# A gated-attention kernel followed by a gelu MLP: one running loop over all batches, no squares on GpSimd, transposing loads issued from SyncE, and buffers of the second phase that wait tile by tile

## The chip, the cores and the metric

One core of a Trainium2 chip runs the whole program. The metric is the time of one execution on the device in microseconds (us), median of several; the profile is of one such execution. A trace's span is some 2 us under the time of its run.

Engines in the profile: PE is TensorE (matmuls), PEld its weight loads, DVE is VectorE, ACT ScalarE, POOL GpSimd, SP SyncE, which issues DMAs. A letter q behind a name is the engine's queue of issues. L225 is line 225 of that kernel, so the same statement has another number in another kernel.

## The reference, cut to what matters

```python
# u, v: (8, 3008, 256)   z: (8, 3008, 64)   w_in: (256, 2048)   w_out: (2048, 256)
scores = (z @ z.transpose(0, 2, 1)) / 3008
attn = np.maximum(scores, 0.0) ** 2
x = (u * (attn @ v)).reshape(8 * 3008, 256)
h = x @ w_in
out = (h / (1 + np.exp(-1.702 * h))) @ w_out
```

## The kernel before: the parts that matter

The first phase works batch by batch. A batch has 72 iterations: two score matmuls (each on 64 rows, so z must lie on partitions 0 to 63 and again on 64 to 127), a relu with eviction (four in five on ScalarE, one in five on VectorE), a square (one in four on GpSimd), and, six iterations later, eight O matmuls.

```python
for b in range(B):
    for k in range(NIT + DPIPE):                  # 72 + 6: the last six only drain
        ...                                       # casts of V for b + 1 at k = 2, 6, 10, 14
        if k == NIT + 1: emit_zt_tr(b + 1, 0)     # 12 transposes into a buffer of the scores
        elif k == NIT + 2: emit_zt_ev(b + 1, 0)   # ScalarE: to ZT, partitions 0 to 63
        elif k == NIT + 3: emit_zt_tr(b + 1, 1)
        elif k == NIT + 4: emit_zt_ev(b + 1, 1)
        elif k == NIT + 5: emit_zt_dup(b + 1)     # DMA: copy to partitions 64 to 127
        if k < NIT: ...                           # sc = scores(k), two buffers
        if 0 <= k - 1 < NIT:
            ...                                   # r = relu(sc): VectorE if tcount % 5 == 0
            if POOL_SQ_EVERY and tcount % POOL_SQ_EVERY == 0:      # 4
                pool.tensor_tensor(ap_, r, r, ALU.mult)
            else:
                dve.tensor_tensor(ap_, r, r, ALU.mult)
        if k - DPIPE >= 0: ...                    # O += ap_ @ V; every 12th: X = O * u on VectorE
    sp.dma_start(xdram[...], X)                   # cut
```

The second phase takes 47 blocks of 512 tokens. Its input XT comes by transposing DMAs from xdram, issued from ScalarE; the first four blocks' (eight DMAs) run already in the second batch of the first phase, as soon as their X is stored.

```python
with (tc.tile_pool(name="pb", bufs=2) as pb, ...):   # takes the place of the first phase's pools
    load_xt(0, act)
    for tb in range(NTB + 1):
        load_xt(tb + 1, act)
        for fg in range(NFG):        # 8 groups: 4 matmuls to hg, sigmoid on ACT, GT = hg * tsg on DVE
            ...
        ...                          # 64 matmuls GT @ W2 of block tb - 1 to yps, ysb, store
```

By default a pool that is opened where others were waits for all users of those.

The names in the profile: ZT is the transposed z, ztp its transposes, sc the scores, r their relu, ap_ the square, O the products with V, X is O * u; hg is h, tsg its sigmoid, GT their product, yps the sums of the output, ysb their copy. The drain is the last six iterations of a batch, in which no new scores are made.

## Time and profile before

| | before |
|---|---|
| time, median of the first 4 runs | 1549.83 us (1549.45 to 1550.1) |
| span of the trace | 1547.7 us |
| first phase, first real scores to last O | 32.7 to 855.7 us |

The share of the whole span that TensorE is busy (95%) hides that it is full inside batches and stands for much of the time between them; the lines that show it are in the prediction. One more list matters, who made TensorE wait in the whole run: columns are total us, times, longest us.

```profile
PE sc L217 <- DMA ZT<-ZT: 43.1, 8, 16.7
...
PE hg L289 <- DVE GT L297: 8.7, 2, 7.9
PE sc L217 <- ACT r L232: 7.6, 10, 1.1
PE sc L217 <- DVE r L230: 3.2, 6, 1.0
```

The copy of ZT leads by far; 16.7 of its 43.1 us are in the start, the rest at the seven borders.

### The profile page before, as it was taken

The page shows a single profiled execution, that of the slowest core. Times are in us where ns is not written, and L with a number is a line of the kernel's source. Part 1 is how long each engine was busy: PE and PEld are TensorE (multiplying, and loading weights), DVE is VectorE, ACT ScalarE, POOL GpSimd, SP SyncE. Part 2 cuts the span into 40 slices and gives each one's busy share as a digit, 9 for nine tenths or more (in the row PEclk, how much of TensorE's full clock was granted, in tenths as well). Part 3 has the DMA queues.
Part 4 walks back from the last instruction along what each step waited for, and adds up shares of the span by engine and source line. Part 5 has one row for each costly group of instructions (what it writes and reads, how often), then busy time and mean ns, then how long its engine had stood idle before and what let it go on. Part 6 is the DMA issues. An engine that isn't in the chain of part 4 may idle for free.

```text
span 1547.7 us, 24671 instructions
## 1 busy us (share of the span) xinstructions
PE 1465.9 (95%) x10464; PEld 917.8 (59%) x10464; DVE 1116.6 (72%) x1117; ACT 892.0 (58%) x869; POOL 282.6 (18%) x152
## 2 busy tenths in 40 slices
PE   2998998999989999999999799999999999999998
PEld 1564564664646656656566466666666666666666
DVE  3875786777767767677687577777777777777775
ACT  2765665666656666566566455565555555555553
POOL 1332332333323323333333000000000000000000
PEclk9998999998989999999999899999999999999999
DMA  9916315115142021121200212111111211211211
GB/s 305 262 32 175 58 40 164 42 48 156 40 121 85 26 78 42 37 68 40 78 29 26 54 55 62 48 59 59 54 57 55 62 49 55 62 49 56 61 35 55
DMA packets 175422, 113.66 MB, mean 73 GB/s; under 512 B 77776, under 2 KB 174032, under 8 KB 175056
## 3 DMA queue, kind: packets, MB, share of 16 engines
q1 hardware_dynamic: 123376, 95.56, 20.9%
q10 hardware_dynamic: 51136, 12.33, 3.9%
q0 software_dynamic: 800, 4.19, 0.8%
q8 instruction: 82, 1.34, 0.4%
q14 instruction: 28, 0.23, 0.1%
HBM read 59.64 MB, written 36.96 MB: 62 GB/s over the span
## 4 chain that ended last, share of the span: by engine, by line
PE 89%; DMA 5%; DVE 2%; ACT 2%; issue 1%; ACTq 1%; SPq 0%; POOL 0%; DVEq 0%; POOLq 0%
PE O L252 34%; PE hg L289 22%; PE yps L314 21%; PE sc L217 11%; DMA ZT<-ZT 2%; ACT r L232 1%; DMA zst<-in_z_dram 1%; DMA xdram<-X 1%; PE ztp L132 1%; DMA w1s<-in_moe_w_in_dram 1%; ACTq L85 1%; DVE r L230 1%; ACT ZT L139 0%; DVE X L260 0%; DVE GT L297 0%
## 5 line engine op out<-in xcount | busy, mean ns | idle before, releaser
L232 ACT ACTIVATE r<-sc 128x1024 f16<-128x1024 f32 x461 | 467.6, 1023 | 300.8 <-PE sc L217 294.4
L296 ACT ACTIVATE tsg<-hg 128x1024 f16<-128x1024 f32 x376 | 379.6, 1023 | 286.8 <-PE hg L289 182.7
L297 DVE TENSOR_TENSOR GT<-hg,tsg 128x1024 f16<-128x1024 f32 x376 | 447.2, 1221 | 114.0 <-ACT tsg L296 111.9
L289 PE MATMUL hg<-XT,W 128*128 128x512 f16 x1504 | 372.8, 380 | 10.1 <-DVE GT L297 8.7
L314 PE MATMUL yps<-W,GT 128*128 128x256 f16 x3008 | 374.1, 273 | 0.0
L314 PEld LDWEIGHTS <-GT 128*128 128x128 f16 x3008 | 294.2, 98 | 94.0
L217 PE MATMUL sc<-ZT 64*128 64x512 f16 x1152 | 236.9, 400 | 55.0 <-DMA ZT<-ZT 43.1
L289 PEld LDWEIGHTS <-W 128*128 128x128 f16 x1504 | 146.6, 98 | 152.5 <-issue 28.2
L217 PEld LDWEIGHTS <-ZT 64*128 64x128 f16 x1152 | 57.4, 93 | 187.1 <-issue 138.1
L230 DVE TENSOR_SCALAR r<-sc 128x1024 f16<-128x1024 f32 x115 | 139.9, 1217 | 26.9 <-PE sc L217 26.7
L320 DVE TENSOR_SCALAR ysb<-yps 128x512 f32<-128x512 f32 x94 | 64.4, 685 | 64.9 <-PE yps L314 64.9
L260 DVE TENSOR_TENSOR X<-O,ru 128x1024 f16<-128x1024 f32 x48 | 58.5, 1218 | 27.6 <-PE O L252 27.6
L139 ACT ACTIVATE ZT<-ztp 64x1536 f16<-64x1536 f16 x16 | 23.0, 1442 | 31.5 <-PE ztp L132 31.5
L110 DVE CAST zst<-zst 128x1536 f16<-128x1536 f32 x8 | 7.7, 959 | 35.9 <-PE ztp L132 21.5
L132 PE MATMUL ztp<-ident,zst 128*64 128x128 f16 x192 | 14.8, 233 | 11.1 <-DVE zst L110 11.1
L182 ACT ACTIVATE V<-vst 128x1536 f16<-128x1536 f32 x14 | 20.2, 1480 | 6.4 <-PE O L252 6.4
L132 PEld LDWEIGHTS <-zst 128*64 128x64 f16 x192 | 12.3, 118 | 14.0 <-DVE zst L110 11.1
L180 DVE CAST V<-vst 128x1536 f16<-128x1536 f32 x14 | 12.9, 956 | 0.0
L296 ACT ACT_TABLE_LOAD x1 | 1.3, 1283 | 13.5 <-DMA xdram<-X 13.5
L158 DVE CAST V<-vst 128x1536 f16<-128x1536 f32 x4 | 3.6, 954 | 7.5 <-DMA vst<-in_v_dram 7.5
L236 POOL TENSOR_TENSOR ap__186<-r 128x1024 f16<-128x1024 f16 x1 | 1.9, 1887 | 21.8 <-ACT r L232 21.8
L236 POOL TENSOR_TENSOR ap__1340<-r 128x1024 f16<-128x1024 f16 x1 | 2.3, 2323 | 15.3 <-ACT r L232 15.3
(1740 smaller groups left out, 1719.3 us busy)
## 6 DMA issues: line engine op xcount, KB each, us to landing
out_dram<-ysb SPq DMA_DIRECT2D x47, 512.0 KB, 2.9
vst<-in_v_dram SPq DMA_DIRECT2D x8, 2944.0 KB, 13.0
ru<-in_u_dram SPq DMA_DIRECT2D x40, 512.0 KB, 3.9
xdram<-X SPq DMA_DIRECT2D x8, 1472.0 KB, 7.7
zst<-in_z_dram SPq DMA_DIRECT2D x8, 736.0 KB, 6.4
ZT<-ZT SPq DMA_DIRECT2D x8, 384.0 KB, 6.2
ru<-in_u_dram SPq DMA_DIRECT2D x8, 384.0 KB, 3.4
w1s<-in_moe_w_in_dram POOLq DMA_DIRECT2D x1, 2048.0 KB, 10.4
```

Source lines behind the costliest of these rows:

```text
L132: pe.transpose(ztp[:DQK, jj, :], zst16[:, j, :], ident)
L139: act.activation(zts[b][:DQK, g * (NJ // 2) * P:(g + 1) * (NJ // 2) * P], ztp[:DQK], AF.Copy, scale=1.0)
L217: pe.matmul(sc[:, g, :], ZT[h0:h0 + DQK, j * P:(j + 1) * P], ZT[h0:h0 + DQK, isup * ISUP:(isup + 1) * ISUP], start=True, stop=True,)
L230: dve.tensor_scalar(r[:, :, :], sc[:, :, :], 0.0, csc, ALU.max, ALU.mult)
L232: act.activation(r[:, :, :], sc[:, :, :], AF.Relu, scale=csc)
L252: pe.matmul(O[:, ib, :], ap_[:, g, ib * P:(ib + 1) * P], V16[:, j, :], start=first, stop=last,)
L260: dve.tensor_tensor(X[:, isup * NIBS:(isup + 1) * NIBS, :], O, ru, ALU.mult)
L289: pe.matmul(hg[:, e, :TBC], W1[:, k, ff * P:(ff + 1) * P], XT[:, k, :TBC], start=(k == 0), stop=(k == NK - 1),)
L296: act.activation(tsg[:, :, :TBC], hg[:, :, :TBC], AF.Sigmoid, scale=1.702 / FSC)
L297: dve.tensor_tensor(GT[:, fg * FFG:(fg + 1) * FFG, :TBC], hg[:, :, :TBC], tsg[:, :, :TBC], ALU.mult,)
L314: pe.matmul(yps[:, s2, :], GT[:, ff, s * P:(s + 1) * P], W2[:, ff, :], start=(ff == 0), stop=(ff == NFF - 1),)
L320: dve.tensor_scalar(ysb[:, yy * 2:yy * 2 + ns2, :], yps[:, :ns2, :], 1.0 / FSC, None, ALU.mult)
```

## The change

Its intent: the pipeline runs on from batch to batch, with the next batch's ZT made early and in a buffer of O; GpSimd does no squares; the transposing loads leave ScalarE's queue; and the second phase's buffers wait only for the tiles whose place they take.

```diff
-POOL_SQ_EVERY = 4
+POOL_SQ_EVERY = 0
-            ztp = ps_sc.tile([P, NJ // 2, P], F16, name="ztp", tag="sc")
+            ztp = ps_o.tile([P, NJ // 2, P], F16, name="ztp", tag="O")
-        for b in range(B):
-            for k in range(NIT + DPIPE):
+        ZT_TR0 = 42
+        ZT_EV0 = 44
+        ZT_TR1 = 55
+        ZT_EV1 = 57
+        ZT_DUP = 58
+        for gk in range(B * NIT + DPIPE):
+            b0, k0 = divmod(gk, NIT)          # scores
+            ...
+            g1 = gk - 1                       # relu, square
+            g2 = gk - DPIPE                   # O, of the batch that g2 falls in
-        tc.tile_pool(name="pb", bufs=2) as pb,                  # and ps_h, ps_y
+        tc.tile_pool(name="pb", bufs=2, reuse_waits="tile") as pb,
-        load_xt(0, act)                                         # and load_xt(tb + 1, act)
+        load_xt(0, sp)
```

(The bodies of the loop are the same statements with other indices.)

More of the change, by code (lines that the diff above doesn't have):

```diff
@@ L168 @@
             dve.tensor_copy(W2, w2s)
-        for b in range(B):
-            _, V16, X, _casts = loads.pop(b)
-            ZT = zts.pop(b)
-            scs = [None] * (NIT + DPIPE)
-            aps = [None] * (NIT + DPIPE)
-            Os = [None] * (NIS + 1)
-            us = [None] * (NIS + 1)
-            for k in range(NIT + DPIPE):
-                if k % 4 == 2 and (b + 1) in loads and loads[b + 1][3]:
-                    o, i_ = loads[b + 1][3].pop(0)
-                    if (k // 4) % 2 == 0:
+        ZT_TR0 = 42
[3 more added lines that the diff above has]
+        ZT_DUP = 58
+        V16d = {}
+        Xd = {}
+        scs = {}
+        aps = {}
+        Os = {}
+        us = {}
+        for gk in range(B * NIT + DPIPE):
+            b0, k0 = divmod(gk, NIT)
+            if b0 < B:
+                if k0 == 0:
+                    _, V16d[b0], Xd[b0], _c = loads.pop(b0)
+                if k0 % 4 == 2 and (b0 + 1) in loads and loads[b0 + 1][3]:
+                    o, i_ = loads[b0 + 1][3].pop(0)
+                    if (k0 // 4) % 2 == 0:
                         dve.tensor_copy(o, i_)
@@ L182 @@
                         act.activation(o, i_, AF.Copy, scale=1.0)
-                if k == PRO_AT:
-                    emit_loads(b + 2)
-                if k == NIT + 1:
-                    emit_zt_tr(b + 1, 0)
-                elif k == NIT + 2:
-                    emit_zt_ev(b + 1, 0)
-                elif k == NIT + 3:
-                    emit_zt_tr(b + 1, 1)
-                elif k == NIT + 4:
-                    emit_zt_ev(b + 1, 1)
-                elif k == NIT + 5:
-                    emit_zt_dup(b + 1)
@@ L195 @@
-                for kq in ((k,) if k < NIT else ()):
-                    isup, jp = divmod(kq, NJP)
-                    if jp == 0:
-                        ru = pa.tile([P, NIBS, D], F32, name="ru", tag="ru")
-                        us[isup] = ru
-                        lo = isup * ISUP
-                        hi = min(S, lo + ISUP)
-                        nfull = (hi - lo) // P
-                        if nfull:
-                            sp.dma_start(
-                                ru[:, :nfull, :],
-                                u[b, lo:lo + nfull * P].rearrange("(n p) c -> p n c", p=P),
-                            )
-                        rem = (hi - lo) - nfull * P
-                        if rem > 0:
-                            sp.dma_start(ru[:rem, nfull, :], u[b, lo + nfull * P:hi].unsqueeze(1))
-                            dve.memset(ru[rem:, nfull, :], 0.0)
-                    sc = ps_sc.tile([P, 2, ISUP], F32, name="sc", tag="sc")
-                    scs[kq] = sc
-                    for g in range(2):
-                        j = 2 * jp + g
-                        h0 = g * DQK
+                if k0 == PRO_AT:
+                    emit_loads(b0 + 2)
@@ new lines @@
+                if k0 == ZT_TR0:
+                    emit_zt_tr(b0 + 1, 0)
+                elif k0 == ZT_EV0:
+                    emit_zt_ev(b0 + 1, 0)
+                elif k0 == ZT_TR1:
+                    emit_zt_tr(b0 + 1, 1)
+                elif k0 == ZT_EV1:
+                    emit_zt_ev(b0 + 1, 1)
+                elif k0 == ZT_DUP:
+                    emit_zt_dup(b0 + 1)
+                isup, jp = divmod(k0, NJP)
+                ZT = zts[b0]
+                if jp == 0:
+                    ru = pa.tile([P, NIBS, D], F32, name="ru", tag="ru")
+                    us[(b0, isup)] = ru
+                    lo = isup * ISUP
+                    hi = min(S, lo + ISUP)
+                    nfull = (hi - lo) // P
+                    if nfull:
+                        sp.dma_start(
+                            ru[:, :nfull, :],
+                            u[b0, lo:lo + nfull * P].rearrange("(n p) c -> p n c", p=P),
+                        )
+                    rem = (hi - lo) - nfull * P
+                    if rem > 0:
+                        sp.dma_start(ru[:rem, nfull, :], u[b0, lo + nfull * P:hi].unsqueeze(1))
+                        dve.memset(ru[rem:, nfull, :], 0.0)
@@ new lines @@
+                sc = ps_sc.tile([P, 2, ISUP], F32, name="sc", tag="sc")
+                scs[gk] = sc
+                for g in range(2):
+                    j = 2 * jp + g
+                    h0 = g * DQK
+                    pe.matmul(
+                        sc[:, g, :],
+                        ZT[h0:h0 + DQK, j * P:(j + 1) * P],
+                        ZT[h0:h0 + DQK, isup * ISUP:(isup + 1) * ISUP],
+                        start=True, stop=True,
+                    )
+            g1 = gk - 1
@@ new lines @@
+            if g1 >= 0 and g1 in scs:
+                sc = scs.pop(g1)
+                r = pr.tile([P, 2, ISUP], F16, name="r", tag="r")
+                tcount += 1
+                if DVE_RELU_EVERY and tcount % DVE_RELU_EVERY == 0:
+                    dve.tensor_scalar(r[:, :, :], sc[:, :, :], 0.0, csc, ALU.max, ALU.mult)
+                else:
+                    act.activation(r[:, :, :], sc[:, :, :], AF.Relu, scale=csc)
+                ap_ = pr.tile([P, 2, ISUP], F16, name="ap_", tag="ap_")
+                aps[g1] = ap_
+                if POOL_SQ_EVERY and tcount % POOL_SQ_EVERY == 0:
+                    pool.tensor_tensor(ap_, r, r, ALU.mult)
+                else:
+                    dve.tensor_tensor(ap_, r, r, ALU.mult)
@@ new lines @@
+            g2 = gk - DPIPE
+            if g2 >= 0 and g2 in aps:
+                b2, k2 = divmod(g2, NIT)
+                isup, jp = divmod(k2, NJP)
+                ap_ = aps.pop(g2)
+                V16 = V16d[b2]
+                if jp == 0:
+                    Os[(b2, isup)] = ps_o.tile([P, NIBS, D], F32, name="O", tag="O")
+                O = Os[(b2, isup)]
+                for g in range(2):
+                    j = 2 * jp + g
+                    for ib in range(NIBS):
+                        first = (jp == 0 and g == 0 and (ib % 2) == 0)
+                        last = (jp == NJP - 1 and g == 1 and (ib % 2) == 1)
@@ L217 @@
                         pe.matmul(
-                            sc[:, g, :],
-                            ZT[h0:h0 + DQK, j * P:(j + 1) * P],
-                            ZT[h0:h0 + DQK, isup * ISUP:(isup + 1) * ISUP],
-                            start=True, stop=True,
-                        )
-                k1 = k - 1
-                if 0 <= k1 < NIT:
-                    sc = scs[k1]
-                    scs[k1] = None
-                    r = pr.tile([P, 2, ISUP], F16, name="r", tag="r")
-                    tcount += 1
-                    if DVE_RELU_EVERY and tcount % DVE_RELU_EVERY == 0:
-                        dve.tensor_scalar(r[:, :, :], sc[:, :, :], 0.0, csc, ALU.max, ALU.mult)
-                    else:
-                        act.activation(r[:, :, :], sc[:, :, :], AF.Relu, scale=csc)
-                    ap_ = pr.tile([P, 2, ISUP], F16, name="ap_", tag="ap_")
-                    aps[k1] = ap_
-                    if POOL_SQ_EVERY and tcount % POOL_SQ_EVERY == 0:
-                        pool.tensor_tensor(ap_, r, r, ALU.mult)
-                    else:
-                        dve.tensor_tensor(ap_, r, r, ALU.mult)
@@ L239 @@
-                k2 = k - DPIPE
-                if k2 >= 0:
-                    isup, jp = divmod(k2, NJP)
-                    ap_ = aps[k2]
-                    aps[k2] = None
-                    if jp == 0:
-                        Os[isup] = ps_o.tile([P, NIBS, D], F32, name="O", tag="O")
-                    O = Os[isup]
-                    for g in range(2):
-                        j = 2 * jp + g
-                        for ib in range(NIBS):
-                            first = (jp == 0 and g == 0 and (ib % 2) == 0)
-                            last = (jp == NJP - 1 and g == 1 and (ib % 2) == 1)
-                            pe.matmul(
-                                O[:, ib, :],
-                                ap_[:, g, ib * P:(ib + 1) * P],
-                                V16[:, j, :],
-                                start=first, stop=last,
-                            )
-                    if jp == NJP - 1:
-                        ru = us[isup]
-                        dve.tensor_tensor(X[:, isup * NIBS:(isup + 1) * NIBS, :], O, ru, ALU.mult)
-                        Os[isup] = None
-                        us[isup] = None
@@ L263 @@
-            sp.dma_start(
-                xdram[b * S:b * S + S0].rearrange("(n p) c -> p n c", p=P),
-                X[:, :NJ - 1, :],
-            )
-            if SREM:
-                sp.dma_start(xdram[b * S + S0:(b + 1) * S].unsqueeze(1), X[:SREM, NJ - 1, :])
+                            O[:, ib, :],
+                            ap_[:, g, ib * P:(ib + 1) * P],
+                            V16[:, j, :],
+                            start=first, stop=last,
+                        )
+                if jp == NJP - 1:
+                    X = Xd[b2]
+                    ru = us.pop((b2, isup))
+                    dve.tensor_tensor(X[:, isup * NIBS:(isup + 1) * NIBS, :], O, ru, ALU.mult)
+                    del Os[(b2, isup)]
+                    if isup == NIS - 1:
+                        sp.dma_start(
+                            xdram[b2 * S:b2 * S + S0].rearrange("(n p) c -> p n c", p=P),
+                            X[:, :NJ - 1, :],
+                        )
+                        if SREM:
+                            sp.dma_start(xdram[b2 * S + S0:(b2 + 1) * S].unsqueeze(1), X[:SREM, NJ - 1, :])
+                        del Xd[b2], V16d[b2], zts[b2]
@@ L270 @@
     with (
-        tc.tile_pool(name="pb", bufs=2) as pb,
-        tc.tile_pool(name="ps_h", bufs=3, space=bass.MemoryType.PSUM) as ps_h,
-        tc.tile_pool(name="ps_y", bufs=2, space=bass.MemoryType.PSUM) as ps_y,
+        tc.tile_pool(name="pb", bufs=2, reuse_waits="tile") as pb,
+        tc.tile_pool(name="ps_h", bufs=3, space=bass.MemoryType.PSUM, reuse_waits="tile") as ps_h,
+        tc.tile_pool(name="ps_y", bufs=2, space=bass.MemoryType.PSUM, reuse_waits="tile") as ps_y,
     ):
         GTs = [None] * (NTB + 1)
-        load_xt(0, act)
+        load_xt(0, sp)
@@ L277 @@
         for tb in range(NTB + 1):
             if tb < NTB:
-                load_xt(tb + 1, act)
+                load_xt(tb + 1, sp)
                 TBC = TBCs[tb]
```

## The prediction

> **What bounds the kernel now.** The page first. Its busy line says that TensorE leads, so the question is where TensorE works at its own pace and where it waits.
>
> ```profile
> PE 1465.9 (95%) x10464; PEld 917.8 (59%) x10464; DVE 1116.6 (72%) x1117; ACT 892.0 (58%) x869; POOL 282.6 (18%) x152
> ...
> L236 POOL TENSOR_TENSOR ap__186<-r 128x1024 f16<-128x1024 f16 x1 | 1.9, 1887 | 21.8 <-ACT r L232 21.8
> ```
>
> No other engine is above 72%. GpSimd holds 144 of the 576 squares, at 1.9 to 2.4 us each. Second, busy time by stretches, cut at the batch borders: the inside of a batch (354 to 444) against a border (234 to 247), the join of the two phases (849 to 868) and the second phase. Columns are the length of the stretch, each engine's busy time with its instructions, then clock, DMA share and GB/s.
>
> ```profile
> 234.00:247.00 13.00, 7.63 (x74) 5.73 (x73) 4.30 (x6) 5.74 (x4) 1.89 (x1) 0.95 0.58 130
> ...
> 354.00:444.00 90.00, 90.00 (x678) 53.86 (x678) 70.26 (x73) 56.83 (x56) 33.96 (x18) 0.98 0.24 72
> ...
> 849.00:868.00 19.00, 9.78 (x73) 6.77 (x72) 4.71 (x6) 4.55 (x5) 1.99 (x1) 0.88 0.29 81
> 868.00:1530.00 662.00, 661.15 (x4386) 428.32 (x4385) 500.53 (x463) 375.73 (x373) 0.00 (x0) 1.00 0.18 54
> ```
>
> Inside a batch TensorE is busy all 90.00 of 90 us, while VectorE is at 78% and ScalarE at 63%: nothing done for those two can shorten it. At the border TensorE has only 7.63 of 13 us. Third, the chain of waits and the timeline, to see what the border is.
>
> ```profile
> 237.31 0.80 PE ztp L132 x12
> 238.13 1.45 ACT ZT L139
> 239.60 7.07 DMA ZT<-ZT
> 246.72 0.62 PE sc L217
> 247.37 1.24 DVE r L230
> ```
>
> ```profile
> 246.72 1.03 PE L217 MATMUL sc<-ZT 64*128 64x512 f16 x2 [5.37 <-DMA ZT<-ZT]
> ...
> 864.03 1.28 ACT L296 ACT_TABLE_LOAD   x1 [13.51 <-DMA xdram<-X]
> ...
> 867.65 6.56 PE L289 MATMUL hg<-XT,W 128*128 128x512 f16 x16 [7.90 <-DVE GT L297]
> ```
>
> The next batch's transposed z is made only while the pipeline drains: transposes, an eviction on ScalarE, then a copy to the other 64 partitions that takes 7 us to land, and TensorE stands 5.4 us for it. Then the pipeline of depth 6 fills again. At the join ScalarE's first sigmoid waits until 864 for the last store of X, although its data (hg) were ready at about 858; TensorE runs 12 matmuls ahead and then stands 7.90 us.
>
> The size of the borders. In the steady stretch eight O matmuls start at 268.30 and those twelve iterations later at 283.94, so 1.303 us an iteration; 72 of them are 93.8 us a batch, with the two transposes (2 x 0.8 us) 95.4. The second eviction of ZT, one a batch, starts at 130.91, 238.13, 342.74, 447.32, about 552.3, 653.01 and 754.18: the batches took 107.2, 104.6, 104.6, 105.0, 100.7 and 101.2 us, which is 11.8, 9.2, 9.2, 9.6, 5.3 and 5.8 over. The first batch (32.7 to 133.6) is 5.5 over, the last (756.9 to 855.7, no transposes) 5.0. Sum 61.4 us of 823. The largest has eight transposing DMA issues on ScalarE's queue in it, 1.1 to 1.8 us each, between 143 and 158.
>
> **What the Trainium skill says.** "SBUF — State Buffer", section "SBUF: two separate sides": VectorE and GpSimd share one port pair, as an exclusive lock, held for the whole instruction, also against a VectorE operation with two SBUF inputs. The trace agrees. A square on VectorE takes 0.68 us alone; the one that began at 203.96 took 2.21, because GpSimd's ran from 203.73 to 205.62. In sum the 432 squares on VectorE take 390.1 us, mean 0.903. "TensorE: Matmul & The Clock Gate", section "What's actually happening": after about 3.4 idle us the array falls to half its clock. The trace agrees: granted clock 0.74 in 133 to 140, and a pair of sc matmuls takes 0.61 to 1.03 us after the wait in place of 0.39. "ScalarE: Activation LUTs", section "What ACT_TABLE_LOAD costs": 1283 ns for any set; here 1283 ns, once at the join. "DMA: Bandwidth & Descriptors", section "Issuing engines are not separate DMA queues": another issuing engine saves only the sequencer's time. Here that is about 1.25 us of ScalarE for each of 94 transposing DMAs.
>
> **The change part by part.**
>
> 1. *Squares all on VectorE.* It gains 144 x 0.68 = 98 us and loses the blocking, 432 x (0.903 - 0.68) = 96 us. Net 2 us of busy time on an engine at 78% where TensorE sets the pace: 0 us.
>
> 2. *One loop over all batches.* An iteration of the next batch follows the last without a drain, and the squares of the last six are consumed beside the first scores of the next. Transposes move to iterations 42 and 55, the copy to 58: at 1.3 us an iteration it has 14 x 1.3 = 18 us, against 7 to land. What goes is the excess of the seven later batches, 61.4 - 5.5 = 55.9 us. The first batch's filling (5.5) and the 32.7 us before it stay. The transposes stay on TensorE, 0.8 us each.
>
> 3. *What comes back.* The work that hid in the border (two evictions of 1.44 us and two casts of 1.48 on ScalarE; two casts of 0.95 and one of 0.96 on VectorE) now stands between relus. Scores have two buffers, so relu has some 2.2 us from ready to needed and takes 1.02 or 1.22: a burst of 1.4 us costs at most some 0.4, and the engine catches up within three iterations (slack of 0.48 us an iteration on ScalarE). The transposes now take one of the two O buffers: at iteration 42 the next O can start only when VectorE has multiplied the last one out (1.22 us plus the queue ahead of it), covered by 0.86 of transposes and 0.43 of scores, so 0 to 1 us. The second set, at 55, finds a free buffer. Estimate from these: 1.5 us a batch, 7 x 1.5 = 10.5 us.
>
> 4. *Buffers of the second phase wait for the tiles whose place they take, not for the whole pools.* At the join, from the last O (855.7) to steady work (867.65), TensorE did 2.8 us of work: 9.2 lost. If the tsg and GT buffers do not lie on the X of the last batch, the path is one hg pair (0.9), perhaps the table load (1.28), sigmoid 1.02 and product 1.22, against 2.6 us of hg work that three buffers allow: 1 to 2 us lost, so 7.5 saved. If they do lie on it, GT still waits for the store and 1 to 2 is saved. I give the first three chances in four: 6 us.
>
> 5. *Transposing loads from SP.* The eight early ones leave ScalarE in the second batch; that gain is already in part 2. In the second phase they delay one sigmoid per block by 1.2 us, but then TensorE is in a run of 49 yps matmuls that needs no sigmoid: 0.
>
> Sum: 55.9 - 10.5 + 6 = 51.4, less 1549.8 gives 1498. The second phase (868 to the end, 680 us) is carried over unchanged.
>
> **The rivals.** *VectorE becomes the bound.* For it: it gets a third more squares and has 20% of the relus, every one able to hold a score buffer. Against: the blocking it sheds is as large as the work it takes, and what it does in an iteration is 0.68 + 1.22/5 + 1.22/12 = 1.03 of 1.30 us. Were it to cost 0.1 us an iteration, 58 us would be lost and the time would be about 1555. *A new wait takes the border's place.* For it: only two score and two O buffers, in order queues, and a cast of z that waits for the transposes: VectorE stood 4.8 us for it at 238.14, which is harmless in a drain and not in a running pipeline. At 5 us a batch in place of 1.5 the time is about 1522. Against: first batch casts, at 43 to 60, cost some 2 to 3 us in all. *The instruction order shifts in the second phase.* The product there runs back to back on VectorE (seven in 8.34 us) while TensorE alternates, and a block takes 14.35 us against 13.65 for 32 x 0.2133 and 64 x 0.1067 (my estimate from the row widths at the pace of the long runs). A ScalarE free of issues might save up to 0.7 x 47 = 33 us, giving 1465. Against: TensorE is in order and its order should be the same.
>
> **Range and chances.** Nearly all of 51 us is idle TensorE time that the timeline shows, and each batch has a term of its own, so the error is mainly part 3 (0.5 to 4 us a batch: minus 7 to plus 17 us) and part 4 (minus 2 to plus 5). That gives 1483 to 1516. The 2% line is 1519, so faster 0.92, same 0.07, slower 0.01.
>
> **What would show it.** Windows of 10 us over the borders should have TensorE at 95% and over, with no 5 us wait for ZT and the clock at 1.0; successive batches should be about 97 us apart; the wait list should lose "sc from DMA ZT" but for the first; squares on VectorE should show 576 at about 0.68 and GpSimd nothing after the start; the first sigmoid should begin within 2 us of the first hg. I am wrong in part 3 if TensorE shows waits for relu of more than 2 us a batch, in part 4 if the first sigmoid or product still ends its wait with the X store, and in part 5 if the blocks of the second phase are not 14.35 us apart.

## The result, and the profile after

| | before | after |
|---|---|---|
| time, median | 1549.45 us (13 runs) | 1483.74 us (1483.21 to 1484.78, 8 runs) |
| span of the trace | 1547.7 us | 1481.5 us |
| last O of the first phase ends | 855.67 us | 800.85 us |
| from there to the end | 692.00 us | 680.65 us |

The ratio is 0.9579 (95% interval 0.9569 to 0.9588). Ratios are the mean time of one kernel's fast runs over that of the other's of the same rounds, so not quite the ratio of the medians. The output is correct.

Of the 66.2 us between the spans, 54.8 came in the first phase and 11.4 after it. The prediction had 55.9 - 10.5 = 45.4 and 6. The engines' busy times of the changed kernel:

```profile
PE 1443.8 (97%) x10464; PEld 913.2 (62%) x10464; DVE 1110.3 (75%) x1261; ACT 891.1 (60%) x869; POOL 2.7 (0%) x8
```

VectorE executes 144 instructions more and is busy 6 us less. The stretches of the changed kernel, in the columns of those of before (the first crosses a batch border near 320, the third is the join):

```profile
234.00:334.00 100.00, 99.36 (x774) 61.31 (x772) 78.87 (x105) 67.70 (x66) 0.00 (x0) 1.00 0.37 102
...
634.00:734.00 100.00, 99.98 (x780) 61.67 (x779) 75.48 (x98) 64.45 (x63) 0.00 (x0) 1.00 0.19 54
...
800.00:824.00 24.00, 22.74 (x137) 13.15 (x136) 20.77 (x18) 16.26 (x16) 0.00 (x0) 1.00 0.32 87
```

Borders can no longer be seen: 99.36 us and more of 100, clock 1.00. What TensorE still waits for:

```profile
PE sc L225 <- DMA ZT<-ZT: 17.3, 1, 17.3
...
PE sc L225 <- ACT r L239: 1.7, 4, 0.7
PE hg L299 <- DVE GT L307: 0.7, 2, 0.4
```

Seven of the eight waits for ZT are gone; the one of the start stays. The last products O * u of the batches begin at 134.15, 230.60, 326.12, 422.25, 518.01, 614.06 and 710.26: batches of 95.5 to 96.5 us, on average 0.6 over the floor of 95.4 that I had worked out, where I had allowed 1.5. At the join, in the changed kernel's timeline:

```profile
795.71 1.28 ACT L306 ACT_TABLE_LOAD   x1
...
801.75 1.02 ACT L306 ACTIVATE tsg<-hg 128x1024 f16<-128x1024 f32 x1 [4.75 <-PE hg L299]
...
802.16 2.94 PE L299 MATMUL hg<-XT,W 128*128 128x512 f16 x12 [0.45 <-DVE X L269]
```

The table load lies beside the last O matmuls, the first sigmoid waits for its data alone, and TensorE stands at most 0.45 us at a time in place of 7.90.

So the direction is right, and 1483.74 lies inside the range of 1483 to 1516, but at its very edge. Some 15 us of gain came from where I had expected none. The experiments look for them.

### The profile page after: what moved, and what is told of

Its sections match the earlier page's. It is cut to its first block, busy times and chain, and to the rows that moved or that the text cites.

```text
span 1481.5 us, 24464 instructions
## 1 busy us (share of the span) xinstructions
PE 1443.8 (97%) x10464; PEld 913.2 (62%) x10464; DVE 1110.3 (75%) x1261; ACT 891.1 (60%) x869; POOL 2.7 (0%) x8
## 4 chain that ended last, share of the span: by engine, by line
PE 95%; DVE 2%; DMA 1%; ACT 1%; SPq 1%; issue 0%; ACTq 0%; DVEq 0%
PE O L260 37%; PE hg L299 23%; PE yps L324 22%; PE sc L225 12%; DMA zst<-in_z_dram 1%; PE ztp L132 1%; SPq L114 1%; ACT r L239 1%; DVE X L269 0%; DVE r L237 0%; DVE GT L307 0%; ACT V L190 0%; SPq L107 0%; DVE W L168 0%; DVE V L188 0%
## 5 line engine op out<-in xcount | busy, mean ns | idle before, releaser
L225 PE MATMUL sc<-ZT 64*128 64x512 f16 x1152 | 227.8, 389 | 19.6 <-DMA ZT<-ZT 17.3
L299 PEld LDWEIGHTS <-W 128*128 128x128 f16 x1504 | 145.9, 97 | 141.9 <-issue 17.8
L225 PEld LDWEIGHTS <-ZT 64*128 64x128 f16 x1152 | 55.9, 93 | 140.8 <-issue 120.8
L132 PE MATMUL ztp<-ident,zst 128*64 128x128 f16 x192 | 14.6, 231 | 11.4 <-DVE zst L110 11.1
L110 DVE CAST zst<-zst 128x1536 f16<-128x1536 f32 x8 | 7.6, 956 | 14.8 <-DMA zst<-in_z_dram 14.7
```

The source lines that it names most:

```text
L132: pe.transpose(ztp[:DQK, jj, :], zst16[:, j, :], ident)
L225: pe.matmul(sc[:, g, :], ZT[h0:h0 + DQK, j * P:(j + 1) * P], ZT[h0:h0 + DQK, isup * ISUP:(isup + 1) * ISUP], start=True, stop=True,)
L299: pe.matmul(hg[:, e, :TBC], W1[:, k, ff * P:(ff + 1) * P], XT[:, k, :TBC], start=(k == 0), stop=(k == NK - 1),)
```

## The experiments

Times are medians, beside the kernel before on the same chip. First each small part was added alone to the kernel before, then each taken alone out of the changed kernel.

**The squares.** Added to the kernel before:

```diff
-POOL_SQ_EVERY = 4
+POOL_SQ_EVERY = 0
```

> The kernel before with nothing changed but all squares on VectorE. Theory A (squares are neutral, TensorE sets the pace inside a batch): 1549 us less 0 to 3 us; the only place for a gain is the first 27 us after the start of the scores, where the changed kernel's TensorE did 176 matmuls in 33 to 60 us against 160. Theory B (GpSimd's blocking of VectorE is what the prediction missed, 9 us of it): 1540 or less. Theory C (VectorE becomes the bound): above 1555.

Measured 1546.01 us against 1549.47: 3.5 us (ratio 0.9973, interval 0.9962 to 0.9984). Close to theory A, a little over its range; TensorE does 178 matmuls between 33 and 60 us in place of 160. Now the same line put back into the changed kernel (0 to 4):

> The changed kernel with every fourth square on GpSimd again. Theory A (relu has slack enough by itself, so bursts cost nothing): 1484 to 1487. Theory B (the bursts of casts and evictions are harmless only because VectorE is no longer blocked for up to 1.6 us at a time): the 9 us of return that I predicted and did not find come back, 1490 to 1496.

Measured 1498.55 us, against 1483.74: 14.8 us, and at once the time that I had predicted for the whole change. Theory A falls, and theory B named too little. (TensorE's instruction order is the same but for a few lines.) In this kernel's trace, just after the border of the first batch, where the casts of V fall in:

```profile
140.94 2.47 POOL L243 TENSOR_TENSOR ap__1386<-r 128x1024 f16<-128x1024 f16 x1 [5.09 <-DVE r L237]
141.58 2.38 DVE L245 TENSOR_TENSOR ap__1401<-r 128x1024 f16<-128x1024 f16 x1
...
144.62 2.20 POOL L243 TENSOR_TENSOR ap__1449<-r 128x1024 f16<-128x1024 f16 x1 [1.20 <-ACT r L239]
144.98 2.38 DVE L245 TENSOR_TENSOR ap__1432<-r 128x1024 f16<-128x1024 f16 x1
147.29 1.21 DVE L237 TENSOR_SCALAR r<-sc 128x1024 f16<-128x1024 f32 x1
...
148.55 0.39 PE L225 MATMUL sc<-ZT 64*128 64x512 f16 x2 [1.56 <-DVE r L237]
```

Two squares on VectorE take 2.38 us each beside squares on GpSimd, where one takes 0.68 alone; the relu behind them in the same queue starts late; the scores have two buffers and TensorE waits 1.56 us for that relu. The same place in the changed kernel, without GpSimd:

```profile
141.17 0.68 DVE L245 TENSOR_TENSOR ap__1432<-r 128x1024 f16<-128x1024 f16 x1
...
142.90 1.22 DVE L237 TENSOR_SCALAR r<-sc 128x1024 f16<-128x1024 f32 x1
...
143.41 0.39 PE L225 MATMUL sc<-ZT 64*128 64x512 f16 x2
```

Over the run, TensorE's wait for VectorE's relu is this with GpSimd's squares, and 0.2 us in one wait without:

```profile
PE sc L225 <- DVE r L237: 10.1, 10, 2.4
PE O L260 <- DVE X L269: 1.8, 3, 0.7
...
PE ztp L132 <- DVE X L269: 1.3, 2, 0.7
```

The waits for X rise from 0.7 to 3.1 us (O and transposes together). No wait of TensorE for a square of GpSimd is in the list. The longest one, 2.43 us, stands behind a cast of V on VectorE that took 2.64 us in place of 0.95, so casts are held up as well as squares. The spans differ by 15.1 us: TensorE's idle time grew by 11.9, about what these waits add (12.3), and its busy time by 3.2 (1447.0 against 1443.8). Matmuls did take longer after that longest wait: the granted clock was 0.62 from 340 to 342 us. Batches are 96.7 to 99.9 us apart.

Is it the blocking, or that a square of 1.9 us comes late to its own O matmuls? In the next run VectorE does all squares, and GpSimd works on something that nobody needs.

```diff
                     dve.tensor_tensor(ap_, r, r, ALU.mult)
+                if tcount % 4 == 0:
+                    scr = pr.tile([P, 2, ISUP], F16, name="scr", tag="scr", bufs=2)
+                    pool.tensor_tensor(scr, r, r, ALU.mult)
```

> The changed kernel, all squares on VectorE as in it, and GpSimd squares every fourth r a second time into a scratch tile that nobody reads; the result is right. If GpSimd's squares cost time because they keep VectorE waiting (a square of 0.69 us that took 2.38 beside one): 10 us or more above 1484, though nobody waits for GpSimd, and squares on VectorE with a mean near 0.85 to 0.9 us. If they cost because their own result came late (1.9 us against 0.69): 1484 to 1486.

Measured 1543.75 us: 60 us lost to work without a reader. The 576 squares on VectorE take 551.4 us (mean 0.957) in place of 390.9 (0.679), and TensorE's wait list says who passes it on:

```profile
PE sc L225 <- DVE r L237: 43.6, 54, 2.8
...
PE O L263 <- DVE X L272: 4.3, 7, 1.0
PE ztp L132 <- DVE X L272: 3.8, 7, 1.0
```

So GpSimd's squaring beside VectorE's is enough to lose time; that its result comes late is not needed. The 60 us are no measure of the 14.8, though: here VectorE also keeps the 144 squares, and it is busy 755.83 of the 827 us from 33 to 860 (91%), so it is near to setting the pace itself. What ties the 14.8 us to VectorE is the wait list of the run before. One thing is mixed in: GpSimd's reading holds the r buffers longer, too (there are seven; TensorE's wait for ScalarE's relu is 1.3 us, so it does not show).

**The waits by tile.** Added to the kernel before; every engine's instruction order is the same, only waits differ:

```diff
-        tc.tile_pool(name="pb", bufs=2) as pb,
+        tc.tile_pool(name="pb", bufs=2, reuse_waits="tile") as pb,     # and ps_h, ps_y
```

> The kernel before with nothing changed but the three pools of the second phase waiting by tile. Instruction order is the same on every engine, only waits differ. My theory after the result: the join costs 9.2 us of standing and some 3 us more because the 16 hg matmuls after it run at half pace (6.56 us in place of 3.4), so 11 us go: 1538. Rival: the half pace is not a consequence of the standing, or the buffers lie on the last X: 1541 to 1548.

Measured 1539.54 us against 1549.47: 9.9 us. Taken out of the changed kernel:

> The changed kernel with the three pools of the second phase waiting for whole pools again. My theory: the join is back with its standing and its half pace, 11 us: 1495. Rival (the changed kernel's join is shorter for another reason, its merged loop): 1484 to 1488.

Measured 1493.31 us: 9.6 us. Both are near the 11 expected, and this part adds up, whatever the rest does. The standing is back, and after it the slow matmuls, in the trace of the latter:

```profile
809.02 1.28 ACT L306 ACT_TABLE_LOAD   x1 [13.49 <-DMA xdram<-X]
...
812.65 2.72 PE L299 MATMUL hg<-XT,W 128*128 128x512 f16 x6 [7.88 <-DVE GT L307]
```

The first six hg matmuls (the view ends there) take 2.72 us, some 0.43 each, where the changed kernel's twelve take 2.94 in all. The granted clock was 0.50 from 808 to 816 us: that is the cold clock that the prediction read at the borders and forgot at the join.

**The queue of the transposing loads.** Added to the kernel before:

```diff
-        load_xt(0, act)          # and load_xt(tb + 1, act)
+        load_xt(0, sp)
```

> The kernel before with nothing changed but the transposing loads issued from SP. Theory A: the second batch loses its extra (11.8 us over the floor against 9.2 and 9.2 in the next two), the second phase keeps 14.35 us a block: 1547, 2 to 3 us less. Rival: a ScalarE free of issues speeds each of 47 blocks by up to 0.7 us: 1515 to 1540.

Measured 1545.55 us against 1549.47: 3.9 us (ratio 0.9973, interval 0.9961 to 0.9984), nearer to A; the rival's 9 us and more are out. Taken out of the changed kernel:

> The changed kernel with the transposing loads issued from ScalarE again. Theory A: eight issues of 1.2 to 1.8 us come between relus in the second batch and stop the scores for 2 to 6 us there, nothing in the second phase: 1486 to 1490. Rival (second phase gains from it): above 1490, blocks longer than 14.35 us.

Measured 1495.77 us: 12.0 us, far over my 2 to 6. The time is in the rival's range, but its reason is not: blocks are 14.36 us apart. In the traces the first phase ends 11.0 us later, and what follows takes 2.0 us longer. Between 134 and 164 us TensorE does 154 matmuls in place of 231, at a mean clock of 0.89: 77 matmuls, ten to an iteration of 1.30 us, are 10 us by estimate. In this run's timeline:

```profile
143.42 8.13 ACTq L85 DMA_TRANSPOSE XT<-xdram  x5
...
151.65 1.02 ACT L239 ACTIVATE r<-sc 128x1024 f16<-128x1024 f32 x1 [8.50 <-DMA XT<-xdram]
...
152.72 0.61 PE L225 MATMUL sc<-ZT 64*128 64x512 f16 x2 [5.76 <-ACT r L239]
```

Five issues hold ScalarE's queue for 8.13 us, not for 5 x 1.25; ScalarE idles 8.50 us before its next relu, and the clock drops. In the changed kernel SP's queue is held by the same eight issues for 4.89 and 6.39 us, and no computing engine stands behind it. What held the issues beyond their 1.25 us is not shown; loads of the next v were under way.

**Early ZT without the merged loop, and late ZT within it.** The kernel before with early ZT, draining each batch as ever:

```diff
-            ztp = ps_sc.tile(..., tag="sc")
+            ztp = ps_o.tile(..., tag="O")
-                if k == NIT + 1:         # + 2, + 3, + 4, + 5
+                if k == 42:              # 44, 55, 57, 58
```

> The kernel before with the next batch's transposes, evictions and copy at iterations 42 to 58 through the O buffers, but with the drain of each batch kept. If the wait for ZT is the larger part of a border (5.4 us standing and a cold clock after it): at least 5 us a border come off, 35 us or more, 1514 or less. If the drain and refilling is a cost of its own: about 3 us a border off, 1530.

Measured 1531.5 us against 1549.28: 17.8 us, the second theory (2.5 us a border). And yet all seven waits for ZT are gone:

```profile
PE sc L217 <- ACT r L232: 19.3, 13, 4.7
PE sc L217 <- DMA ZT<-ZT: 17.7, 1, 17.7
...
PE sc L217 <- DVE r L230: 6.2, 11, 1.0
```

The wait for ZT lost 25 us, and the waits for relu rose from 10.8 to 25.5, 4.7 of that in one place where transposing issues held ScalarE. The new wait is the filling of the pipeline: with no O work to do, TensorE makes scores faster than two buffers can be relued. The changed kernel with late ZT:

```diff
-        ZT_TR0 = 42     # ZT_EV0 44, ZT_TR1 55, ZT_EV1 57, ZT_DUP 58
+        ZT_TR0 = 66     # 67, 68, 69, 70
```

> The changed kernel with the next batch's transposes, evictions and copy moved to iterations 66 to 70 of 72, so that the copy cannot land before the next batch's first scores. If the wait for ZT was the main part of a border: 4 to 6 us a border, so 7 x 5 = 35 us, 1519. If the drain and refilling was, and the six pending O iterations can cover the wait: under 2 us a border, 1484 to 1498.

Measured 1486.88 us: 3.1 us for seven borders. The instruction order made at build time puts the pending O matmuls ahead of the next scores, and they cover the landing of ZT (four O groups run from 127.85 us on, the copy lands at 130.12, the next scores start at 130.69). So the wait for ZT, the largest line of the list of before, costs little where other work is ready (3.1 us here), and taking it away gives only a part (17.8 us) where the drain stays.

**The merged loop alone.** The changed kernel with all three other parts taken back:

> The changed kernel with only the merged loop left: squares shared with GpSimd, transposing loads from ScalarE, second phase waiting for whole pools. Additions to the kernel before gave 3.5 (squares), 9.9 (waits by tile) and 3.9 us (loads from SP); taken out of the changed kernel the same three cost 14.8, 9.6 and 12.0. If the parts simply add, as my prediction assumed, what is left for the loop is 66 - 17.3 = 49 us: 1501. If squares and loads matter only once TensorE has no standing time to hide them: 1484 + 36.4 = 1520, so the loop alone gives 29.

Measured 1517.32 us against 1549.08: 31.8 us (expected by the second theory 29, by the adding one 49). Added one by one to the kernel before, the four parts make 31.8 + 3.5 + 9.9 + 3.9 = 49.1 us; together they made 65.7. The 16.6 us between are the squares (14.8 against 3.5) and the loads (12.0 against 3.9). By themselves these differences sum to 19.4; some of it is counted twice, since both parts lengthen the second batch. That standing time in the drain had covered the squares is my reading. For the loads there is a rival that no run separates: the order in ScalarE's queue. In the kernel before, the eight issues stand as two, one, one, one and three between relus; with the running loop and the loads on ScalarE, five stand in a row.

**A better version.** In the trace, TensorE is busy 640.00 of 640 us from 824 to 1464, and yet a block takes 14.35 us. The 13.65 of the prediction cannot be had from the trace: in the long runs hg matmuls start 0.2158 us apart and yps matmuls 0.1092, so 32 and 64 of them take 13.9 us. VectorE's products run back to back in the middle of each block, seven in 8.33 us or 1.19 each; there the sets of four hg matmuls start some 1.20 us apart (1000.57, 1001.81, 1003.00, 1004.18), where the paces above give 1.12 with the yps matmuls between. No wait is listed for it. So the hg matmuls were spread evenly among the yps matmuls:

```diff
                 for fg in range(NFG):
                     ...                                # 4 hg matmuls, sigmoid, product
+                    if tb >= 1:
+                        emit_y(tb - 1, fg * 8, fg * 8 + 8)   # 8 of the 64 yps matmuls of the block before
-                ...                                    # the 64 in one go
```

> The changed kernel with the second phase written so that each group of four hg matmuls is followed by eight yps matmuls of the block before. A block then takes 32 x 0.2158 + 64 x 0.1092 = 13.9 us (paces of the long runs in the trace) in place of 14.35 if VectorE's seven products back to back set the pace of the group now: 46 x 0.45 = 21 us, 1463. Rival: the 14.35 is TensorE's own pace with so many switches between shapes, then 1484 or more.

Measured 1463.44 us: 20.3 us less than the changed kernel, where 21 were expected; ratio to before 0.9443 (interval 0.9427 to 0.9459). The half blocks are 6.95 us apart on VectorE, so a block is 13.9, as the paces above give, and the products no longer touch each other:

```profile
1003.01 1.23 DVE L329 TENSOR_TENSOR GT<-hg,tsg 128x1024 f16<-128x1024 f32 x1 [0.51 <-ACT tsg L328]
1004.56 0.69 DVE L306 TENSOR_SCALAR ysb<-yps 128x512 f32<-128x512 f32 x1 [0.33 <-PE yps L299]
...
1011.51 0.69 DVE L306 TENSOR_SCALAR ysb<-yps 128x512 f32<-128x512 f32 x1 [0.33 <-PE yps L299]
```

**And the wait of the start.** As that run, with the first copy of ZT issued from ScalarE:

```diff
-            emit_zt_dup(b)                # sp.dma_start
+            emit_zt_dup(b, act)           # first batch only
```

> As the run with the even interleaving, and the first batch's copy of ZT issued from ScalarE, where it does not queue behind loads. It was issued at 27.2 us although its source was ready at 15.4, and TensorE stood 17.3 us. If only that queue held it: landed at some 22 us, 8 to 10 us less than the run beside it, about 1454. Rival: the copy waits for the DMA engines, which are busy with the loads (share 1.03), as well: 0 to 3 us less.

Measured 1464.24 us, 0.8 more than without. Both theories miss. The copy did land early: scores begin at 23.40 us in place of 32.85. The wait went elsewhere, whole:

```profile
PE O L260 <- DVE ap__164 L245: 10.1, 1, 10.1
PE sc L225 <- DMA ZT<-ZT: 8.4, 1, 8.4
```

The first square stands in VectorE's queue behind the cast of the second batch's z, which begins at 31.71 when its load has landed, and behind a cast of weights. To gain from the early copy, those two casts would have to come later as well; that was not run.

## Why the prediction was right, and where it was not

*Part 1, squares all on VectorE: "Net 2 us of busy time on an engine at 78% where TensorE sets the pace: 0 us."* The step that failed. Its sum was exact: 390.9 us of squares after, 390.1 before. The conclusion was wrong, because what TensorE waits for is one relu behind one square or cast blocked for 1.7 us (10.1 us in ten waits), and not VectorE's sum. The term was 14.8 us in the changed kernel, where casts stand in the queue of a pipeline that runs on, and 3.5 in the kernel before. I had read the evidence from the steady stretch of before (TensorE at 90.00 of 90 us), in which no cast falls.

*Part 2, one loop: "What goes is the excess of the seven later batches".* Right in size: the borders are gone, batches are 0.6 us over the floor. But I told them as a wait for ZT: with early ZT and the drain kept 17.8 us were gained, with the loop as well 31.8, so the drain and the filling cost 14.0 by themselves. That the loop alone brings 31.8 us and not 45.4 (55.9 less the 10.5 of part 3) shows how much of this rests on parts 1 and 5.

*Part 3, what comes back: "1.5 us a batch".* With GpSimd's squares in place, batches are 96.7 to 99.9 us apart in the trace, on average 2.8 us over the floor; without them 0.6. My figure lay between; the bursts did return, but part 1 took them away.

*Part 4, waits by tile: "6 us".* Too small: 9.6 and 9.9 measured. The mechanism, the favourable one of the two, was right; the missing term is the matmuls at half pace after 7.9 us of standing.

*Part 5, loads from SP: "that gain is already in part 2" and "In the second phase ... 0".* Nearly right for the second phase: the blocks are 14.35 us apart as foretold, and 2.0 us are lost there with the loads on ScalarE. The value in the first phase was hidden in the excess of one batch, and is most of the 12.0 us once the pipeline runs and five issues stand in a row.

*The rivals.* VectorE as the bound: no, 75% and almost no wait. A new wait in the border's place: no in the changed kernel, yes (2.2 us a batch more) as soon as GpSimd squares again. A shifted order in the second phase: no, and of the loss it named, up to 0.7 us a block, 0.45 was real and was had by spreading the matmuls; the rest came of the 13.65.

*The range* held 1483.74 by 0.7 us, and that is partly luck: it was drawn from parts 3 and 4 and had no room for the 14.8 us of part 1. The centre, 1498, is the time of the change without its part on the squares (1498.55), by luck too: two errors of opposite sign, in the traces 39.8 us in the first phase for the 45.4 predicted, and 11.2 after it for 6.

## What to carry to other kernels

Taking a standing wait out of the pacing engine can make small delays on the others count: GpSimd's squares cost 3.5 us before and 14.8 after. So price each part in the pipeline that will be there, not in the one that is. The sum of an engine's busy time can stay the same while its longest single instruction shrinks, and here, with two score buffers, it was the longest that TensorE waited for. The transposing loads were better issued from a queue behind which no computing instruction stands (3.9 and 12.0 us).

## What the Trainium skill lacked or had wrong

- "SBUF — State Buffer", section "SBUF: two separate sides", is right on the lock, but gives no price in a whole kernel: here 2.38 us for a square of 0.69, and 60 us for 144 GpSimd squares that nobody reads, on a VectorE then 91% busy. It lacks the remark that the sum can hide it (390.1 us shared, 390.9 alone).
- "DMA: Bandwidth & Descriptors", section "Issuing engines are not separate DMA queues", calls the sequencer's time for a DMA "usually small relative to the DMA itself". Here an issue took 1.25 us of the 2.6 from its start to its landing (medians of the 94 transposing loads of the kernel before), five transposing issues held ScalarE's queue for 8.13 us, and moving the issues to SP was worth 12.0 us.
- "Perfetto Trace Analysis", section "Identifying the Most-Contended Engine", warns off matmul busy time because pipelined instructions "look smaller in the trace". Here it misled the other way, and the prediction leaned on it too much: at 640.00 of 640 us busy, the second phase still gave 20.3 us to another order of the same matmuls.
- No page that I read tells what waiting by tile in place of by pool is worth where one phase's buffers take the place of another's: 9.6 and 9.9 us here, with the half-pace matmuls after the standing.
